# First layer and attention in nine blocks of 512 tokens instead of twelve of 384

## The chip, the cores and the metric

The kernel runs on one core of a Trainium2 chip. The metric is the device time of one execution in microseconds (us), without transfers from the host. The engines are TensorE (PE, its weight loads PEld), VectorE (DVE), ScalarE (ACT), GpSimd (POOL) and SyncE (SP, which issues all DMAs here).

## The reference

Attention over 8 batches of 8 heads, 576 tokens each, head width 64, with keys and values averaged over groups of 8 tokens (72 pooled rows per head), and then two expert layers over the 4608 tokens of width 512:

```python
k_p = k.reshape(B, H, Sp, pool, D).mean(axis=3)          # Sp = 72, pool = 8
v_p = v.reshape(B, H, Sp, pool, D).mean(axis=3)
scores = scale * np.matmul(q, k_p.transpose(0, 1, 3, 2))
scores = scores - np.max(scores, axis=-1, keepdims=True)
attn = np.exp(scores)
attn = attn / (np.sum(attn, axis=-1, keepdims=True) + 1e-09)
x = np.matmul(attn, v_p)                                 # -> 4608 x 512
h = x @ w_in; r = np.maximum(h, 0.0); x = (r * r) @ w_out         # first layer, d_ff 2048
gate = 1.0 / (1.0 + np.exp(-(x @ w_gate)))                        # second layer, d_ff 1536
out = (gate * (x @ w_val)) @ w_out2
```

The weights arrive as float64. The kernel turns them into float32 by integer operations on their halves.

## The kernel before

**Matmuls.** Each float32 operand of the two layers is split into a rounded high part and a remainder, and a product is three matmuls (high·high, high·low, low·high: `PASSES`). Tokens lie along the free dimension. In the first layer a block of `NA` = 384 tokens meets 16 slices `f` of the hidden width: `mm1` (line 791) makes the 128 hidden rows of slice `f` with 12 matmuls of 384 columns, ACT and DVE form the squared ReLU and split it (`relu`, `sq`, `ghi`, `glo`, lines 834 to 847), and `mm2` (line 800) adds their part of the output with 12 more. There are 12 blocks.

**Order of the blocks.** `SEGS` lists block 0 with slices 0 to 7, block 1 with all 16, block 0 with slices 8 to 15, and then blocks 2 to 11. So the 32 weight slices of the first layer are converted while the first two segments run. A conversion is a DMA, an integer addition on POOL, one ACT operation, four on DVE (lines 246 to 257) and a split on ACT and DVE (lines 273 and 277). The slices stay in SBUF for the whole layer.

**Attention.** For a block and half of the heads (`hf`), `attend` takes tiles of 128 tokens: scores on PE (line 443), maximum, exponential and scaling (`softmax1` to `softmax3`), a transposition of the result (on PE for blocks 0 and 1, line 528, by DVE and DMAs for the later ones, lines 511 and 522), and the product with the pooled values (line 544). A tile of block `b` holds the 32-token groups `a::NTA` of the block, a stride of three groups. From block 3 on, `softmax1` subtracts the maximum on DVE (line 467), one ACT operation takes the exponential of all four heads, and DVE sums. In the first three blocks (`FEW`) ACT takes it head by head, with the maximum as its bias and the sum as a by-product (line 496). Pooling of keys and values is done once per batch by DVE (line 381), or by PE for the first two batches (line 632).

**Second layer.** It works in blocks of 768 tokens with 384-column matmuls for the gate and value products (line 1181) and 512-column matmuls for the output (line 1296). It begins when the first layer ends.

**What sets the order.** Every operation is entered into `Plan` with an engine, a guessed duration, what it depends on, the buffers that it takes and gives, and a rank. `Plan.run` plays them through and so fixes the order of each engine's instructions; on the chip an engine works through its list in that order and waits where a semaphore isn't there yet. `T0` and `TF` are the planned start of the first layer and the planned length of a slice. Products of slice `f` are ranked `TI(f)` for `mm1` and 1.5 slices later for `mm2`, so that `mm2(f)` stands behind `mm1(f+1)`.

## Time and profile before

| | us |
|---|---|
| median of 3 runs (1782.91 to 1785.81) | 1784.85 |
| the profiled execution | 1785.78 |
| its span, first to last instruction | 1784.0 |
| PE busy in the span | 1752.6 (98%) |
| DVE busy | 1160.5 (65%) |
| ACT busy | 774.6 (43%) |
| mean granted clock of TensorE | 0.996 |

The span is what the trace covers; 1.8 us of the execution lie around it. A busy share is a mean over stages with different limits, so the rows below are taken stage by stage. Busy PE time contains the modelled end of each pipelined matmul: how fast a stream of matmuls really goes is read from the starts.

### The profile page before, as it was taken

How to read it: one execution, taken by the hardware profiler on the slowest of the kernel's cores; microseconds unless marked ns; L12 is line 12 of the kernel's file. 1: busy time of each engine (PE TensorE's matmuls, PEld its weight loads, DVE VectorE, ACT ScalarE, POOL GpSimd, SP SyncE). 2: the span in 40 equal slices, each digit the busy share in tenths (PEclk: the TensorE clock that was granted, in tenths of full speed). 3: DMA queues.
4: the chain of work that ended last, by engine and by line, in shares of the span. 5: the costliest groups of instructions: out<-in, count | busy, mean ns of one | idle time of the engine just before them, and what ended most of it. 6: DMA issues, size and time to landing. Idle time of an engine off the chain costs nothing.

```text
span 1784.0 us, 26488 instructions
## 1 busy us (share of the span) xinstructions
PE 1752.6 (98%) x9720; PEld 1636.1 (92%) x9720; DVE 1160.5 (65%) x2310; ACT 774.6 (43%) x1718; POOL 245.9 (14%) x186
## 2 busy tenths in 40 slices
PE   8898999999999999999999999999999999999999
PEld 3697889999999999999999999999999999999998
DVE  7999788788677886653357555555555655655554
ACT  6666533333333334333245444455444444444442
POOL 2500100000000000000023111212111212111100
PEclk9999999999999999999999999999999999999999
DMA  9632345343243442312022222223333333333321
GB/s 285 214 97 74 92 97 147 97 130 95 80 112 103 123 105 77 92 45 63 13 67 82 71 71 83 72 83 116 115 107 107 119 107 119 118 104 103 103 79 50
DMA packets 194658, 179.15 MB, mean 100 GB/s; under 512 B 105184, under 2 KB 143584, under 8 KB 194528
## 3 DMA queue, kind: packets, MB, share of 16 engines
q1 hardware_dynamic: 194528, 177.46, 33.8%
q8 instruction: 76, 1.25, 0.3%
q14 instruction: 54, 0.44, 0.1%
HBM read 119.80 MB, written 48.76 MB: 94 GB/s over the span
## 4 chain that ended last, share of the span: by engine, by line
PE 89%; DVE 3%; ACT 1%; DMA 1%; issue 1%; SPq 1%; POOL 0%; DVEq 0%; ACTq 0%; POOLq 0%
PE acc L800 20%; PE h L791 19%; PE h L1181 17%; PE acc L1296 17%; PE att L1181 8%; PE acc L1181 4%; PE att L544 2%; PE att L443 2%; DVE g L847 0%; DMA kv<-in_k_dram 0%; POOL raw L236 0%; SPq L427 0%; DVE kp L381 0%; DMA raw<-in_moe_w_out_dram 0%; DVE vp L381 0%
## 5 line engine op out<-in xcount | busy, mean ns | idle before, releaser
L791 PE MATMUL h<-x,in 128*128 128x384 f32 x2304 | 438.6, 339 | 7.9 <-DVE x L785 3.0
L800 PE MATMUL acc<-g,out 128*128 128x384 f32 x2304 | 439.3, 338 | 5.1 <-DVE g L847 2.5
L791 PEld LDWEIGHTS h<-x,in 128*128 128x128 f32 x2304 | 401.0, 189 | 19.4 <-issue 7.4
L800 PEld LDWEIGHTS acc<-g,out 128*128 128x128 f32 x2304 | 400.6, 188 | 18.1 <-DVE g L847 5.0
L834 ACT ACTIVATE r<-h 128x384 f32<-128x384 f32 x192 | 93.9, 489 | 262.1 <-PE h L791 257.0
L1296 PE MATMUL acc<-in,p 128*128 128x512 f32 x648 | 182.5, 390 | 0.0
L1296 PE MATMUL acc<-out,p 128*128 128x512 f32 x648 | 182.1, 389 | 0.0
L840 DVE TENSOR_TENSOR r<-r,h 128x384 f32<-128x384 f32 x160 | 87.8, 549 | 132.9 <-ACT r L834 131.9
L1203 ACT ACTIVATE res<-h 128x384 f32<-128x384 f32 x144 | 70.6, 491 | 211.3 <-PE h L1181 210.5
L844 ACT ACTIVATE g<-r 128x384 fp32r<-128x384 f32 x192 | 100.8, 525 | 108.5 <-DVE r L840 97.3
L1296 PEld LDWEIGHTS acc<-out,p 128*128 128x128 f32 x648 | 121.6, 188 | 25.7
L1296 PEld LDWEIGHTS acc<-in,p 128*128 128x128 f32 x648 | 121.4, 188 | 24.1
L847 DVE TENSOR_TENSOR g<-r,g 128x384 fp32r<-128x384 f32 x192 | 112.8, 587 | 42.8 <-ACT g L844 41.9
L236 POOL INT64_ADD raw<-raw x40 | 47.0, 1174 | 646.3 <-DMA raw<-in_moe_w_out_dram 176.6
L1212 DVE TENSOR_TENSOR res<-res,acc 128x384 f32<-128x384 f32 x72 | 39.7, 551 | 125.6 <-PE acc L1181 125.6
L1322 DVE TENSOR_TENSOR o<-o,acc 128x512 f32<-128x512 f32 x72 | 49.5, 688 | 94.9 <-PE acc L1296 74.1
L1262 ACT ACTIVATE p<-res 128x384 fp32r<-128x384 f32 x144 | 75.3, 523 | 70.8 <-DVE res L1256 70.6
L1014 POOL TENSOR_TENSOR yt<-yf,yt 128x768 f32<-128x768 f32 x32 | 62.1, 1942 | 273.6 <-DVE out L1041 272.3
L1181 PE MATMUL h<-out,in 128*128 128x384 f32 x432 | 98.4, 335 | 0.0
L1181 PE MATMUL h<-in,out 128*128 128x384 f32 x432 | 98.1, 334 | 0.3 <-DVE res L1212 0.3
L1181 PE MATMUL h<-in,in 128*128 128x384 f32 x432 | 98.1, 334 | 0.0
L1181 PE MATMUL h<-out,out 128*128 128x384 f32 x432 | 98.0, 334 | 0.0
(147 smaller groups left out, 2647.6 us busy)
## 6 DMA issues: line engine op xcount, KB each, us to landing
yf<-y_dram SPq DMA_DIRECT2D x16, 1536.0 KB
o_part<-o SPq DMA_DIRECT2D x72, 256.0 KB
o<-o_part SPq DMA_DIRECT2D x72, 256.0 KB
y_dram<-y SPq DMA_DIRECT2D x48, 192.0 KB
w_dram<-t SPq DMA_DIRECT2D x36, 256.0 KB
w2s<-w_dram SPq DMA_DIRECT2D x36, 256.0 KB
out_dram<-o SPq DMA_DIRECT2D x36, 256.0 KB
raw_w<-in_moe_w_in_dram SPq DMA_DIRECT2D x15, 512.0 KB
```

The lines of the kernel that those rows point to most:

```text
L791: nc.tensor.matmul(out=h[:, 0:n], lhsT=w[:, a, kk * 128:(kk + 1) * 128], rhs=xs[kk][:, c], start=(kk == 0 and i == 0), stop=(kk == KT - 1 ...
L800: nc.tensor.matmul(out=y_ps[m][:, 0:NA], lhsT=w[:, a, m * 128:(m + 1) * 128], rhs=g_t[f][:, c], start=(f == f0 and i == 0), stop=(f == f1 ...
L834: nc.scalar.activation(out=r, in_=st["h"][:, 0:NA], func=ACTF.Relu)
L840: nc.vector.tensor_tensor(out=st["r"], in0=st["r"], in1=st["h"][:, 0:NA], op=ALU.mult)
L844: nc.scalar.activation(out=g[:, 0], in_=st["r"], func=ACTF.Copy)
L847: nc.vector.tensor_tensor(out=g_t[f][:, 1], in0=st["r"], in1=g_t[f][:, 0].bitcast(F32), op=ALU.subtract)
L1014: nc.gpsimd.tensor_tensor(out=t, in0=q(a), in1=q(c), op=ALU.subtract)
L1181: nc.tensor.matmul(out=st[which, z][:, 0:HN], lhsT=w[:, wa, col:col + 128], rhs=ys[y, k2][:, yc], start=(first[z] == m and k2 == 0 and j = ...
L1203: nc.scalar.activation(out=new((which, key)), in_=st[which, z][:, 0:HN], func=ACTF.Copy)
L1262: nc.scalar.activation(out=p_t[fi][:, 0, h * HN:(h + 1) * HN], in_=st["gate", key], func=ACTF.Copy)
L1296: nc.tensor.matmul(out=o_ps[i], lhsT=p_t[f][:, a, i * 128:(i + 1) * 128], rhs=wslot[c, "out", f][:, w], start=(f == 0 and j == 0), stop=(f ...
L1322: nc.vector.tensor_tensor(out=st2["o"], in0=st2["o"], in1=o_ps[i], op=ALU.add)
```

## The change

`NA` becomes 512, so that there are nine blocks, and every matmul of the first layer has 512 columns. A tile of 128 tokens is now 128 adjacent tokens. Columns of a block stand in the order (32-token group, tile, token), which is undone when the block's output is copied out of PSUM (`tail_y`). Seven of the nine blocks lie in two batches; a tile that does is scored in two pieces, and `attn_v` walks the rectangles that `runs` returns. The softmax by heads on ACT is used for all blocks; the minus sign of the maximum comes from the reduction, and the scale is put into the keys when they are placed. `mm2(f)` is ranked 2.5 slices after `mm1(f)` and three buffers hold `g`. The planner's durations and lead times are adapted. The second layer keeps 384 columns (`HN`).

```diff
-    NA = 384
+    NA = 512
-    L2, L2H, LN, LNH, LP, LQ = 73.0, 31.0, 77.0, 35.0, 26.0, 18.0
+    L2, L2H, LN, LNH, LP, LQ = 92.0, 40.0, 96.0, 44.0, 26.0, 18.0
-    T0, TF, TG = 42.0, 4.25, 8.4
+    T0, TF = 44.0, 5.55
+    def runs(i, j):
+        res = []
+        if i % 128:
+            res.append((i % 128 // 32, 4, i // 128, i // 128 + 1))
+        if -(-i // 128) < j // 128:
+            res.append((0, 4, -(-i // 128), j // 128))
+        if j % 128:
+            res.append((0, j % 128 // 32, j // 128, j // 128 + 1))
+        return res
...
     def softmax1(b, hf, a):
...
-        nc.vector.tensor_reduce(out=m, in_=p, op=ALU.max, axis=AX.X)
-        nc.vector.tensor_scalar(out=m, in0=m, scalar1=-scale / POOL, scalar2=None, op0=ALU.mult)
+        nc.vector.tensor_reduce(out=m, in_=p, op=ALU.max, axis=AX.X, negate=True)
...
         for off, n, be, _ in parts(b):
-            for j in range(2):
-                nc.tensor.matmul(
-                    out=p[64 * j:64 * j + 64, off:off + n],
+            for g0, g1, a0, a1 in runs(off, off + n):
+                for j in range(2):
+                    nc.tensor.matmul(
+                        out=pv[64 * j:64 * j + 64, g0:g1, a0:a1],
...
-            if b < FEW:
-                o = op("dve", 0.57, lambda a=a: softmax1_few(b, hf, a), [o], r + 1)
-                o = op("act", 1.25, lambda a=a: softmax2_few(b, hf, a), [o], r + 2, give=(bank[0],))
-                o = op("dve", 0.78, lambda a=a: softmax3_few(b, hf, a), [o], r + 3)
-            else:
-                o = op("dve", 0.87, lambda a=a: softmax1(b, hf, a), [o], r + 1, give=(bank[0],))
-                o = op("act", 0.34, lambda a=a: softmax2(b, hf, a), [o], r + 2)
-                o = op("dve", 1.25, lambda a=a: softmax3(b, hf, a), [o], r + 3)
+            o = op("dve", 0.44, lambda a=a: softmax1(b, hf, a), [o], r + 1)
+            o = op("act", 2.0, lambda a=a: softmax2(b, hf, a), [o], r + 2, give=(bank[0],))
+            o = op("dve", 0.78, lambda a=a: softmax3(b, hf, a), [o], r + 3)
...
-            rank = t + 1.5 * TF
-            need = [o, w_ready["out", f]]
+            rank = t + 2.5 * TF
+            need = [o, w_ready["out", f]] + ([w_last["out", f - 1]] if f > f0 else [])
...
+            o_y = y.rearrange("p (a g t) -> p g a t", a=NTA, g=4)
+            i_y = y_ps[m].rearrange("p (g a t) -> p g a t", a=NTA, g=4)
-                nc.scalar.activation(out=y, in_=y_ps[m][:, 0:NA], func=ACTF.Copy)
+                nc.scalar.activation(out=o_y, in_=i_y, func=ACTF.Copy)
...
-    HN = NA
+    HN = 384
```

On PE, in block 1 (slices 3 to 5; `in_` and `out_` are the two weight slices, `acc` the four output banks), the list before has:

```order
L791 MATMUL h<-x,in_465 128x384 x12
L800 MATMUL acc_1173<-g,out_483 128x384 x3
L800 MATMUL acc_1182<-g,out_483 128x384 x3
L800 MATMUL acc_1191<-g,out_483 128x384 x3
L800 MATMUL acc_1198<-g,out_483 128x384 x3
L791 MATMUL h<-x,in_525 128x384 x12
```

and the list of the change, from slice 2 of the same block:

```order
L777 MATMUL h<-x,in_497 128x512 x12
L786 MATMUL acc_1286<-g,out_433 128x512 x3
L786 MATMUL acc_1294<-g,out_433 128x512 x3
L786 MATMUL acc_1300<-g,out_433 128x512 x3
L786 MATMUL acc_1310<-g,out_433 128x512 x3
L777 MATMUL h<-x,in_577 128x512 x12
```

Before, `out_483` is slice 2, right behind `mm1` of slice 3; now `out_433` is slice 0, behind `mm1` of slice 2. The matmuls have 512 columns where they had 384.

On DVE, at the end of the first segment, where the last weight that this segment needs (`w_out` of slice 7: `out_1038`, now `out_1065`) gets its remainder, the list before has:

```order
L785 TENSOR_TENSOR x<-xf,x 128x384 x2
L503 TENSOR_SCALAR z<-z 128x4
L504 RECIPROCAL z<-z 128x4
L505 TENSOR_TENSOR e_81<-e_81,z 128x4x72
L847 TENSOR_TENSOR g<-r,g 128x384
L277 TENSOR_TENSOR out_1038<-t_w,out_1038 128x512
```

and the list of the change:

```order
L771 TENSOR_TENSOR x<-xf,x 128x512
L256 SCALAR_TENSOR_TENSOR t_w<-raw_w,t_w 128x512
L833 TENSOR_TENSOR g<-r,g 128x512
L390 TENSOR_REDUCE kp<-kv 72x64
L771 TENSOR_TENSOR x<-xf,x 128x512
L276 TENSOR_TENSOR out_1065<-t_w,out_1065 128x512
```

The weight's place on DVE is nearly the same (row 160 before, row 158 now), while the block that it serves has a third more tokens.

On ACT, in a later block (`e_80` and `e_81` are the two buffers of a softmax tile), the list before has:

```order
L472 ACTIVATE e_80<-e_80 128x4x72
L834 ACTIVATE r<-h 128x384
L844 ACTIVATE g<-r 128x384
L834 ACTIVATE r<-h 128x384
L844 ACTIVATE g<-r 128x384
L472 ACTIVATE e_81<-e_81 128x4x72
```

and the list of the change:

```order
L486 ACTIVATE e_80,z<-att,m 128x72 x4
L820 ACTIVATE r<-h 128x512
L486 ACTIVATE e_81,z<-att,m 128x72 x4
L830 ACTIVATE g<-r 128x512
L403 ACTIVATE kpT_79<-att 64x72 x2
L820 ACTIVATE r<-h 128x512
```

One operation per tile has become four, ahead of a `relu` on which PE's next use of that bank depends.

## Rows read from the trace of the kernel before

**Rows 1.** Windows by stage: length, busy PE, PEld, DVE, ACT, POOL, clock, DMA.
```profile
0.00:38.88 38.88, 30.23 (x109) 13.14 (x109) 27.14 (x62) 23.26 (x78) 9.85 (x14) 0.96 1.09 279
38.88:102.64 63.76, 56.27 (x334) 45.86 (x331) 62.15 (x105) 45.86 (x125) 25.34 (x21) 0.95 0.59 191
102.64:180.91 78.27, 70.79 (x394) 67.34 (x392) 73.66 (x150) 48.59 (x118) 4.46 (x4) 0.98 0.37 95
180.91:224.21 43.30, 42.56 (x242) 38.80 (x243) 33.47 (x79) 23.95 (x64) 5.40 (x3) 1.00 0.31 82
224.21:958.31 734.10, 731.07 (x4319) 701.22 (x4319) 509.34 (x1068) 267.47 (x562) 59.60 (x54) 1.00 0.33 90
958.31:1784.00 825.69, 821.68 (x4333) 769.69 (x4332) 454.70 (x851) 365.49 (x775) 141.24 (x93) 1.00 0.30 96
```

**Rows 2.** Timeline of PE, first layer: start, length, what, count.
```profile
899.11 2.24 PE L791 MATMUL h<-x,in 128*128 128x384 f32 x12
...
944.87 2.24 PE L791 MATMUL h<-x,in 128*128 128x384 f32 x12
```

**Rows 3.** Timeline of PE, output products of the second layer.
```profile
992.19 0.84 PE L1296 MATMUL acc<-out,p 128*128 128x512 f32 x3
...
998.99 0.84 PE L1296 MATMUL acc<-out,p 128*128 128x512 f32 x3
```

**Rows 4.** Waits of PE, 38.88 to 102.64: total, times, longest.
```profile
PE att L443 <- ACT qT L716: 2.9, 1, 2.9
PE att L528 <- DVE e L505: 1.9, 1, 1.9
PE h L791 <- DVE x L785: 1.8, 1, 1.8
```

**Rows 5.** Waits of PE, 102.64 to 224.21.
```profile
PE h L791 <- DVE in L277: 2.1, 3, 1.0
PE h L791 <- ACT in L273: 2.1, 2, 1.5
PE acc L800 <- ACT out L273: 1.7, 1, 1.7
```

**Rows 6.** Waits of PE, 224.21 to 958.31.
```profile
PE acc L800 <- DVE g L847: 2.5, 6, 0.7
```

**Rows 7.** Windows in the start, up to the last conversions: columns as rows 1.
```profile
24.55:100.10 75.55, 66.85 (x366) 50.32 (x364) 73.08 (x133) 54.84 (x159) 28.58 (x23) 0.93 0.71 215
100.10:191.92 91.82, 83.39 (x471) 78.66 (x469) 85.16 (x176) 58.75 (x151) 7.77 (x4) 0.98 0.34 88
```

**Rows 8.** Lines of DVE, 24.5 to 102.64: count, busy us, mean ns, idle before.
```profile
L252 DVE SCALAR_TENSOR_TENSOR t_w<-raw_w,t_w 128x512 uint32<-128x512 uint32 x14 | 12.1, 864 | 0.1
...
L847 DVE TENSOR_TENSOR g<-r,g 128x384 fp32r<-128x384 f32 x8 | 6.1, 759 | 0.1
L277 DVE TENSOR_TENSOR out<-t_w,out 128x512 fp32r<-128x512 f32 x8 | 5.4, 681 | 0.0
L505 DVE TENSOR_TENSOR e<-e,z 128x288 f32<-128x288 f32 x9 | 4.7, 524 | 0.3
L381 DVE TENSOR_REDUCE kp<-kv 72x64 f32<-72x512 f32 x4 | 4.2, 1058 | 0.0
```

**Rows 9.** Timeline of PE: scores, two tiles, in halves and whole.
```profile
71.10 1.20 PE L443 MATMUL att<-kpT,qT 128*64 128x144 f32 x16
...
162.99 1.14 PE L443 MATMUL att<-kpT,qT 128*128 128x144 f32 x8
```

**Rows 10.** Timeline of PE: the product with the values, halves and whole.
```profile
101.19 1.52 PE L544 MATMUL att<-aT,vp 72*64 72x192 f32 x16 [0.21 <-ACT aT L536]
...
829.35 1.51 PE L544 MATMUL att<-aT,vp 72*64 72x384 f32 x8
```

**Rows 11.** Timeline of ACT: a tile's four exponentials, and what follows.
```profile
140.97 0.32 ACT L496 ACTIVATE e<-att,m 128x72 f32<-128x72 f32 x1 [1.12 <-DVE m L487]
...
142.30 0.49 ACT L834 ACTIVATE r<-h 128x384 f32<-128x384 f32 x1
```

**Rows 12.** Lines of DVE, 224.21 to 890: the subtraction that goes.
```profile
L467 DVE TENSOR_TENSOR e<-att,m 128x288 f32<-128x288 f32 x49 | 22.4, 458 | 1.7
```

More of the change, by code (lines that the diff above doesn't have):

```diff
@@ L160 @@
     scale = 1.0 / float(D) ** 0.5
+    kscale = scale / POOL
     def pool(name, bufs=1, **kw):
@@ L404, in prep @@
                              take=("kp",) if j == 0 else (), give=("kv",)))
-            o = op("pe", 0.12, lambda pr=pr: tr(pr), ds, rank, take=("att",), give=("kp",), at=0)
             prev = k_users[be - 2, 2 * hf + pr]
+            o = op("pe", 0.12, lambda pr=pr: tr(pr), ds + prev, rank, take=("att",), give=("kp",), at=0)
             k_ready[be, 2 * hf + pr] = op("act", 0.25, lambda pr=pr: place(pr), [o] + prev, rank, give=("att",))
@@ L434, in q_trans @@
         for pr in range(2):
-            nc.vector.transpose(out=qT_t[b, hf][:, pr, a], in_=q_t[b, hf][:, pr, a::NTA, :])
+            nc.vector.transpose(out=qT_t[b, hf][:, pr, a], in_=q_t[b, hf][:, pr, 4 * a:4 * a + 4, :])
     def scores(b, hf, a, bank):
@@ L441, in scores @@
             for off, n, be, _ in parts(b):
-                p0, pn = off * 128 // NA, n * 128 // NA
+                p0, p1 = max(0, off - 128 * a), min(128, off + n - 128 * a)
+                pn = p1 - p0
+                if pn <= 0:
+                    continue
                 nc.tensor.matmul(
@@ L455, in new_e @@
         if u % 2 == 0:
-            e_first[0] = moe.tile([128, 2, 4 * 96], F32, tag="g", name="e", bufs=2)
+            e_first[0] = moe.tile([128, 2, 4 * 96], F32, tag="g", name="e", bufs=3)
         return e_first[0][:, u % 2]
@@ L496, in softmax2_few, with softmax3 @@
             nc.scalar.activation(
-                out=e[:, h, 0:SP], in_=p[:, h * SP:(h + 1) * SP], func=ACTF.Exp, scale=scale / POOL,
+                out=e[:, h, 0:SP], in_=p[:, h * SP:(h + 1) * SP], func=ACTF.Exp,
                 bias=m[:, h:h + 1], accum_out=z[:, h:h + 1])
-    def softmax3_few(b, hf, a):
+    def softmax3(b, hf, a):
         e = e_view(b, hf, a)[:, :, 0:SP]
@@ L520, in a_move @@
             nc.sync.dma_start(
[L521 removed]
+                out=aT_t[b, hf][32 * j:32 * j + w, :, NG * g:NG * (g + 1)],
                 in_=T_t[b, hf][32 * g:32 * g + w, :, j].rearrange("p h a t -> p h (a t)"))
@@ L716, in ev @@
                 nc.scalar.activation(
-                    out=out_of(pr).rearrange("p a g t -> p g a t"),
-                    in_=st["p"][:, 0:NA].rearrange("p (g a t) -> p g a t", g=4, a=NTA), func=ACTF.Copy)
-            o = op("pe", 0.4, tr, loads[NTA * (pr // 2):NTA * (pr // 2 + 1)] + consts, rank + 5 + pr, take=(bank[0],),
+                    out=out_of(pr).rearrange("p a g t -> p (a g t)"), in_=st["p"], func=ACTF.Copy)
+            o = op("pe", 0.5, tr, loads[NTA * (pr // 2):NTA * (pr // 2 + 1)] + consts, rank + 5 + pr, take=(bank[0],),
                    give=takes if pr == KT - 1 else ())
-            res.append(op("act", 0.37, ev, [o], rank + 6 + pr, take=(out_take(pr),) if out_take(pr) else (),
+            res.append(op("act", 0.58, ev, [o], rank + 6 + pr, take=(out_take(pr),) if out_take(pr) else (),
                           give=(bank[0],)))
@@ L757 @@
     q1 = early_q(1, t1 - Q1, 0.5,
-                 [lambda: att.tile([128, 2, H, D], F32, tag="T", name="rows1"),
-                  lambda: att.tile([128, 1, H, D], F32, tag="kv", name="rows1", bufs=3)],
-                 ("T", "kv"), q1_out, lambda pr: {0: "qT", 2: "q"}.get(pr), [("att", 2)] * KT, [c1])
+                 [q0_get(-2), q0_get(-1)], (w1_tag(n1 - 4), w1_tag(n1 - 3)), q1_out, lambda pr: {0: "qT", 2: "q"}.get(pr), [("att", 2)] * KT, [c1])
     early_kv(1, v, n1 - 11, t1 - P1 + V1L, K1B, [c2], False)
@@ L808, in expert1 @@
         for kk in range(KT):
-            o = op("act", 0.41, lambda kk=kk: x_hi(b, kk), [x_kept[b, kk]], t0 - 60, take=(f"x{kk}",))
-            xr.append(op("dve", 0.47, lambda kk=kk: x_lo(b, kk), [o], t0 - 60, give=((f"xf{kk}", xf_owner[b, kk]),)))
+            o = op("act", 0.6, lambda kk=kk: x_hi(b, kk), [x_kept[b, kk]], t0 - 60, take=(f"x{kk}",))
+            xr.append(op("dve", 0.67, lambda kk=kk: x_lo(b, kk), [o], t0 - 60, give=((f"xf{kk}", xf_owner[b, kk]),)))
         for f in range(f0, f1):
@@ L825, in expert1 @@
                 for kk in range(KT):
-                    o = op("pe", 0.52, lambda kk=kk, l1=l1: l1([kk]), [o, xr[kk], w_ready["in", f]], t,
+                    o = op("pe", 0.68, lambda kk=kk, l1=l1: l1([kk]), [o, xr[kk], w_ready["in", f]], t,
                            take=("h",) if kk == 0 else (), give=give if kk == KT - 1 else ())
             else:
-                o = op("pe", 2.08, lambda l1=l1: l1(range(KT)), [w_ready["in", f]] + xr, t, take=("h",), give=give)
+                o = op("pe", 2.72, lambda l1=l1: l1(range(KT)), [w_ready["in", f]] + xr, t, take=("h",), give=give)
             w_last["in", f] = o
@@ L867, in expert1 @@
             else:
-                o = op("pe", 2.08, lambda f=f: [mm2(f, f0, f1, m) for m in range(KT)], need, rank, give=("g",))
+                o = op("pe", 2.72, lambda f=f: [mm2(f, f0, f1, m) for m in range(KT)], need, rank, give=("g",))
             w_last["out", f] = o
@@ L978, in y_prep @@
         st = {}
-        blks = {x for x in range(t0 // NA, (t0 + TN) // NA)}
+        blks = {x for x in range(t0 // NA, -(-(t0 + TN) // NA))}
         def load():
```

70 lines of the change are left out of this document (26 added, 44 removed).

## The prediction, on record before the changed kernel ran

> **What bounds the kernel now.** I read the windows by stage first, then the starts of PE's matmuls in each stage, PE's waits, and last the lines of DVE and ACT for the stage that waits. The windows [rows 1] are cut where PE's work changes: 38.88 is the first matmul of the first layer, 102.64 lies in the last products of segment 0, 180.91 in the first ones of segment 2, 224.21 is the start of block 2, and 958.31 the first matmul of the second layer. From 224.21 on the reader is to see a PE that hardly rests: 731.1 of 734.1 us and 821.7 of 825.7 busy, at granted clock 1.00. What counts there is the number of matmuls and the time from one start to the next. The start is another matter. Between 38.88 and 224.21 PE is idle for 7.5 + 7.5 + 0.7 = 15.7 us, and the granted clock is 0.95 and 0.98 in the first two windows, which by itself can cost at most 63.8 x 0.05 + 78.3 x 0.02 = 4.8 us. Its waits there are for queries, a scaled softmax tile, the split x and for weight slices [rows 4, 5], all of which come from DVE or from ACT operations that feed it or are fed by it. DVE is the engine without air: 73.1 of 75.6 us up to the remainder of the weight that segment 0 needs last, 85.2 of 91.8 us from there to the last weight [rows 7]. Part of its work is stretched there: the bit operation at line 252 has a mean of 864 ns and the split at line 847 one of 759 [rows 8].
>
> **The change part by part.**
>
> *Matmuls of the first layer.* In a run of products without attention, 22 groups of 12 lie between the two starts shown: (944.87 - 899.11) / 264 = 173.3 ns for 384 columns [rows 2]. The output products of the second layer have 512 columns and another weight tile for each matmul too, as the first layer will: (998.99 - 992.19) / 30 = 226.7 ns [rows 3]. At the full clock of 2.4 GHz, 384 columns are 160.0 ns and 512 are 213.3, so both carry the same 13.3 ns on top, and a third more columns cost 30.8% more time. Before there are 12 x 16 x 24 = 4608 matmuls, 798.7 us; now 9 x 16 x 24 = 3456, 783.4 us. This term is **-15.3 us**, all of it on the path, since PE is the bound for most of the layer.
>
> The Trainium skill has a rule that speaks against this term (page "TensorE: Matmul & The Clock Gate", section "Back-to-back issue gap"): for a single warm stream the gap is the columns at 2.4 GHz plus about 2.5 ns. By it, as an estimate, 1152 matmuls fewer would give 2.9 us and not 15.3, and the sum below would end some 12 us higher. This case's trace disagrees with its size: it has 13.3 ns at both widths [rows 2, 3]. I go by the rows.
>
> *The start: segment 0.* DVE's list up to the last weight of segment 0 has 158 places where it had 160. In it are one key pooling more (1.06 us), two more softmax tiles to scale (0.52 each) with their maxima, eight splits of g and six of x that are a third longer (at most 8 x 0.25 us for g, somewhat less in all for x), and twelve small multiplications of the maxima less [rows 8]. Bounds are +2 and +7 us; I take +6, nearer the upper one, because the list is worked off without a gap. PE's own work in this segment grows by 192 x (226.7 - 173.3) = 10.2 us and by some 2.4 us for two more tiles of attention, an estimate from the length of such groups [rows 9, 10]. So PE gets 12.6 us more work in a stage that DVE lengthens by 6: its waits and cold time shrink by **6.6 us**, from 7.5 idle and up to 3.2 of clock. The number of weights doesn't change; what changes is that each, once there, gives PE a third more to do.
>
> *The start: segments 1 and 2.* Here PE waits 8.2 us, mostly for weights [rows 1, 5]. DVE needs 91.8 us for the last sixteen slices [rows 7], and its list is 153 places long now against 157, with two longer kinds in it: say 97 us. PE's work over segment 1 goes from 66.6 to 87.0 us plus attention (4.2 us before: 78.3 - 7.5 - 66.6; 5.6 with a third more). PE thus comes to the weights later than DVE has them, up to the last two or three, and there the second product helps, which stands behind two further first products. I leave 2.5 us of waits: **-5.7 us**. The ends are 0 and, with all clock loss gone, -9.8.
>
> *Before the first matmul.* Block 0 has eight tiles to go through softmax instead of six, and the first half of the heads, with which `mm1` can begin, needs four where it needed three. One more set of four exponentials for each half of the heads, 142.30 - 140.97 = 1.33 us on ACT [rows 11], lies on this path with its maximum and scaling: bounds 0 (PE has pooling to do meanwhile) and +4; I take **+2**.
>
> *Attention on PE.* The number of tiles stays 72 and so do the columns of the value product. A tile in two pieces costs the same as a whole one (1.20 and 1.14 us for two tiles), and a value product in halves as much as a whole one (1.52 and 1.51) [rows 9, 10]. But `runs` now makes pieces of 64 columns, which the trace doesn't show: two in each of blocks 1, 3, 5 and 7, times four (half and head pair), 32 pairs. The 16 pieces in rows 9 take 1.20 us, 75 ns each for 144 columns; by columns a piece of 64 would need 33 ns. If it can't follow its neighbour faster than those 75 ns, a pair of heads with two passes each loses 4 x 42 ns, 5.4 us in all. The other end is 0, or a little below since value products are grouped into 18 rounds and not 24. I take **+1**.
>
> *DVE and ACT later on.* The subtraction (458 ns a tile [rows 12]) and two reductions leave DVE, four exponentials with their sums instead of one come to ACT, 1.33 us a tile. DVE has 509 of 734 us busy and ACT 267 after 224.21 [rows 1], and what hides both is PE's stream. PE's waits there are 2.5 us, for g [rows 6]. With the second product a slice later g has 12 x 226.7 x 2 = 5.4 us more time, so these waits could go; new ones at block starts are as likely. Cost 0, bounds -3.0 and the slower rival below. DMAs for attention move the same bytes in fewer pieces, off the path. The second layer is left as it is: 0.
>
> *Sum*: -15.3 - 6.6 - 5.7 + 2 + 1 = -24.6 us. From the profiled execution, 1785.8 us, that is 1761.2; the median of the runs is 0.9 lower than this execution, and I forecast **1761 us**.
>
> **The rivals.**
>
> *The start gives nothing.* DVE's chain of conversions stretches with the block (longer splits, more tiles) and PE finds the same holes. For it: DVE is over 90% busy throughout the start. Against it: the number of weight operations is fixed, and they are most of the list. Time: 1785.8 - 15.3 + 2 + 1 = 1773.5 us. Chance 14%.
>
> *The cost goes by columns.* If the first layer's matmuls kept their 451 ns per thousand columns, 512 columns would take 231.1 ns, the term of 15.3 us would vanish, and the time be 1776 us. For it: the first layer's own stream at 512 columns is in no row. Against it: rows 3, with the same operand types. Chance 4%. By the gap rule of the Trainium skill (page "TensorE: Matmul & The Clock Gate", section "Back-to-back issue gap"), as an estimate, 12.4 of the 15.3 us would be missing, which is close to this case.
>
> *More than forecast.* All idle and cold time of the start goes and so do the later waits: -15.3 - 20.5 - 3.0 = -38.8, or 1747; a middle of this case is 1751. Chance 8%.
>
> *Slower: the exponentials hold PE.* From block 3 on there are 48 tiles whose bank of scores is now held until ACT has done its four exponentials, and each set stands ahead of a `relu` on ACT's list. If PE then finds the h bank or the scores' bank taken, it waits. The price: PE must lose (24.6 + 3.6) / 48 = 0.59 us a tile before the kernel is slower by 0.2%; at 0.65 us a tile the time is 1792 us. For it: ACT's list shows the four operations ahead of `relu`. Against it: in the first three blocks the same form runs, at 1.33 us a tile, and no wait there is for it as large [rows 4, 5]; and the bank that `relu` and the square free is needed again only after three further groups of twelve, 3 x 2.72 = 8.2 us. Chance 4%.
>
> That the matmuls don't get their 512 columns is excluded by the instruction list.
>
> **How the numbers follow.** The forecast has 70%, its own range is 1754 to 1769: the bounds of segment 0, of the pieces and of the first matmul add up to about 7 on either side. The others have 14, 4, 8 and 4. To leave out no more than 2 in 10 the range takes in the case without a gain in the start, the one by columns with its own scatter, and most of the low case: 1750 to 1779. A change under 0.2%, 3.6 us, can hardly be told from none for this kernel. All cases but the last are faster by more than that; for pieces that add up worse than thought I move a few points: faster 0.93, the same 0.03, slower 0.04.
>
> **What would show it.** The first layer's two matmul lines with 1728 entries each, 2.72 us from one group of twelve to the next; PE's idle time between its first matmul of the first layer and the start of block 2 at 3 to 6 us, where it was 15.7; that first matmul at 39 to 42 us; the last products of segment 0 at about 108; and the first matmul of the second layer at 934 rather than 958. DVE should lose some tens of microseconds of busy time and ACT gain some, without either showing in the end. The prediction is wrong if groups of twelve take 2.77 us, if PE's waits in the start stay at 15 us with DVE's weights as their cause, or if after the start waits for ACT's exponentials or for `relu` appear in tens of microseconds.

## The result and the profile after

The changed kernel takes 1765.93 us (median of 4 runs, 1764.18 to 1766.26) against 1785.03 us of the kernel before on the same chip. The ratio is 0.9893, with a 95% interval of 0.9876 to 0.991. The forecast was 1761 us in a range of 1750 to 1779. The profiled execution took 1764.18 us with a span of 1762.4, so the span fell by 21.6 us where the working had 24.6. Several terms of that working were off by more than 3 us, in both directions, and most of what follows is about those.

The windows by stage of the changed kernel (length; busy PE, PEld, DVE, ACT, POOL; granted clock, DMA share, GB/s) answer to [rows 1]. The cuts are the first matmul of the first layer, the end of segment 0, the start of block 2, and the first matmul of the second layer:

```profile
0.00:41.24 41.24, 31.08 (x122) 15.46 (x123) 21.97 (x51) 23.13 (x88) 11.29 (x15) 0.96 1.07 271
41.24:117.09 75.85, 70.47 (x335) 49.25 (x333) 70.58 (x118) 55.85 (x146) 25.07 (x19) 0.95 0.49 166
117.09:261.25 144.16, 141.36 (x661) 113.13 (x659) 105.30 (x215) 87.47 (x224) 7.24 (x6) 0.98 0.32 83
261.25:926.78 665.53, 665.08 (x3168) 539.38 (x3167) 438.40 (x824) 272.37 (x744) 59.68 (x54) 1.00 0.35 96
926.78:1762.40 835.62, 827.79 (x4345) 774.79 (x4343) 455.84 (x853) 366.25 (x775) 139.09 (x92) 0.99 0.29 96
```

Read the first column against the second. From 261.25 to 926.78 PE rests 0.45 us in all; before it rested 3.0 us in the same part of the kernel. In the start it still rests 5.4 + 2.8 us, where it was 7.5 + 8.2. And the second layer, which nobody touched, is 835.6 us long and was 825.7.

The timeline of PE in a run of products (start, length, line, what, count) answers to [rows 2]:

```profile
869.66 2.88 PE L786 MATMUL acc<-g,out 128*128 128x512 f32 x12
872.38 2.88 PE L777 MATMUL h<-x,in 128*128 128x512 f32 x12
875.10 2.88 PE L786 MATMUL acc<-g,out 128*128 128x512 f32 x12
```

From one start to the next it is 2.72 us, 226.7 ns a matmul. Each of the two lines has 1728 entries in the list of groups.

The waits of PE from 41.24 to 261.25 (total, times, longest), which answer to [rows 4, 5]:

```profile
PE h L777 <- DVE x L771: 3.3, 1, 3.3
PE att L518 <- DVE e L495: 2.3, 3, 1.7
PE att L518 <- ACT qT L705: 0.9, 1, 0.9
PE att L537 <- ACT aT L526: 0.9, 1, 0.9
PE h L777 <- DVE in L276: 0.7, 1, 0.7
```

The waits for weights have shrunk from 5.9 us [rows 5] to 0.7. The largest wait is one of the first slice's matmuls for the split of x, 3.3 us from 51.6 on; before it was 1.8 [rows 4]. After 261.25 there is one wait of 0.4 us; the 2.5 us for g [rows 6] are gone.

Two groups of attention in the timeline of PE, a score product of two whole tiles and a value product of 32 pieces, answer to [rows 9, 10]:

```profile
421.43 1.14 PE L455 MATMUL att<-kpT,qT 128*128 128x144 f32 x8
474.23 1.99 PE L537 MATMUL att<-aT,vp 72*64 72x256 f32 x32
```

The 32 pieces of the second row (16 of them of 64 columns, though the row prints one form) cover 512 tokens of the block in 1.99 us; before, 384 tokens took 1.51 [rows 10], and a third more of that is 2.01.

### The profile page after: what moved, and what is told of

Its sections match the earlier page's. It is cut to its first block, busy times and chain, and to the rows that moved or that the text cites. A ratio compares the mean times of both kernels' runs of the same rounds, so it can differ in the third digit from the quotient of the medians.

```text
span 1762.4 us, 24051 instructions
## 1 busy us (share of the span) xinstructions
PE 1735.8 (98%) x8624; PEld 1492.0 (85%) x8624; DVE 1092.1 (62%) x2058; ACT 805.1 (46%) x1974; POOL 242.4 (14%) x186
## 4 chain that ended last, share of the span: by engine, by line
PE 93%; DMA 1%; DVE 0%; ACT 0%; issue 0%; SPq 0%; ACTq 0%
PE h L777 22%; PE acc L786 21%; PE h L1169 17%; PE acc L1284 17%; PE att L1169 9%; PE acc L1169 4%; PE att L537 2%; PE att L455 2%; DMA y_dram<-y 0%; DVE vp L390 0%; DMA q<-in_q_dram 0%; PE att L399 0%; PE att L518 0%; DVE in L276 0%; DVE y L868 0%
## 5 line engine op out<-in xcount | busy, mean ns | idle before, releaser
L777 PE MATMUL h<-x,in 128*128 128x512 f32 x1728 | 427.0, 396 | 4.3 <-DVE x L771 3.7
L786 PE MATMUL acc<-g,out 128*128 128x512 f32 x1728 | 421.7, 393 | 0.0
L777 PEld LDWEIGHTS h<-x,in 128*128 128x128 f32 x1728 | 323.1, 189 | 79.6 <-DVE x L771 5.1
L786 PEld LDWEIGHTS acc<-g,out 128*128 128x128 f32 x1728 | 321.3, 188 | 70.7 <-issue 3.9
L820 ACT ACTIVATE r<-h 128x512 f32<-128x512 f32 x144 | 86.1, 598 | 268.7 <-PE h L777 262.8
L826 DVE TENSOR_TENSOR r<-r,h 128x512 f32<-128x512 f32 x112 | 76.5, 683 | 131.1 <-ACT r L820 130.8
L833 DVE TENSOR_TENSOR g<-r,g 128x512 fp32r<-128x512 f32 x144 | 102.6, 713 | 52.7 <-ACT g L830 51.6
L830 ACT ACTIVATE g<-r 128x512 fp32r<-128x512 f32 x144 | 91.1, 633 | 69.4 <-DVE r L826 67.6
L1169 PE MATMUL h<-in,in 128*128 128x384 f32 x432 | 99.3, 337 | 3.8 <-ACT res L1191 3.8
L486 ACT ACTIVATE e<-att,m 128x72 f32<-128x72 f32 x272 | 83.3, 321 | 39.9 <-DVE m L477 39.7
```

Of the source, the lines that this page charges most:

```text
L486: nc.scalar.activation(out=e[:, h, 0:SP], in_=p[:, h * SP:(h + 1) * SP], func=ACTF.Exp, bias=m[:, h:h + 1], accum_out=z[:, h:h + 1])
L777: nc.tensor.matmul(out=h[:, 0:n], lhsT=w[:, a, kk * 128:(kk + 1) * 128], rhs=xs[kk][:, c], start=(kk == 0 and i == 0), stop=(kk == KT - 1 ...
L786: nc.tensor.matmul(out=y_ps[m][:, 0:NA], lhsT=w[:, a, m * 128:(m + 1) * 128], rhs=g_t[f][:, c], start=(f == f0 and i == 0), stop=(f == f1 ...
L820: nc.scalar.activation(out=r, in_=st["h"][:, 0:NA], func=ACTF.Relu)
L826: nc.vector.tensor_tensor(out=st["r"], in0=st["r"], in1=st["h"][:, 0:NA], op=ALU.mult)
L830: nc.scalar.activation(out=g[:, 0], in_=st["r"], func=ACTF.Copy)
```

## The experiments

Each run was compared with the kernel before on its own chip, whose median lay between 1784.9 and 1786.2 us. "After" is the changed kernel, 1765.93 us.

**What the matmuls cost.** In `e2_cols256` each matmul of `mm1` becomes two of 256 columns, so there are 1728 matmuls more and the columns stay the same. (The two halves share one accumulation, so the hidden rows have other values.)

```diff
-            nc.tensor.matmul(
-                out=h[:, 0:n], lhsT=w[:, a, ...], rhs=xs[kk][:, c], ...)
+            for s in (slice(0, n // 2), slice(n // 2, n)):
+                nc.tensor.matmul(
+                    out=h[:, s], lhsT=w[:, a, ...], rhs=xs[kk][:, c, s], ...)
```

> The changed kernel with each matmul of mm1 issued as two of 256 columns: 1728 more matmuls, the same columns. Theory (about 13.3 us per thousand matmuls, whatever their width): a pair takes 240 ns where one took 226.7, +23 us against the changed kernel, 1789 us. Rival (the cost goes by columns): no change, 1766 us. With a fixed cost of 2.5 ns a matmul it would be +4 us, 1770 us.

Measured: 1785.61 us (ratio 1.0002, 0.9991 to 1.0013), 19.7 more than after. Blocks 3 to 7, from the first matmul of block 3 to that of block 8, are windows in which PE doesn't rest at all; first after, then this run:

```profile
362.69:839.74 477.05, 477.05 (x2268) 385.96 (x2267) 300.88 (x579) 188.86 (x519) 36.92 (x34) 1.00 0.35 97
```

```profile
369.40:858.76 489.36, 489.36 (x3228) 437.06 (x3227) 301.01 (x581) 188.57 (x519) 36.02 (x33) 1.00 0.35 95
```

960 matmuls more cost 12.3 us, 12.8 ns each, at clock 1.00 in both. So a matmul has a fixed price of about 13 ns beside its columns, as [rows 2, 3] had it, and the rival by columns falls. The 19.7 us over the whole kernel are a little under the theory's 23. The 2.5 ns that the Trainium skill gives (page "TensorE: Matmul & The Clock Gate", section "Back-to-back issue gap") are there the price of an isolated matmul; for a stream with a weight load for each matmul, as here, the section lets both count and has some 131 ns at 512 columns. The prediction left that out. The 226.7 ns measured here agree with neither figure, and the measurement decides.

**What the later second product is worth.** `e3_lag15` takes the lag back in the changed kernel; `e5_before_lag25` gives it to the kernel before, with a third buffer for g.

```diff
 (e3, in after)                     (e5, in before)
-            rank = t + 2.5 * TF    -            rank = t + 1.5 * TF
+            rank = t + 1.5 * TF    +            rank = t + 2.5 * TF
```

> The changed kernel with the second product ranked 1.5 slices after the first again instead of 2.5 (three buffers of g stay). Theory (most of the gain at the start comes from more matmul work per weight, and in the later blocks the waits for g were 2.5 us before): +1 to +4 us against the changed kernel, 1767 to 1770 us, with waits of the second product for g's remainder or for weights. Rival (the later second product is what hides the start): +6 us or more, with the time lost ahead of block 2.

> Twelve blocks of 384 tokens and the old softmax, as before; only the second product stands 2.5 slices behind the first one (1.5 before), with a third buffer for g. Theory (the longer lag is what fills the holes of segments 1 and 2, whatever the block size): PE's idle time between its first matmul of the first layer and block 2 falls from 15.7 us to 8 or less, block 2 starts some 6 to 8 us earlier than at 224.21, the waits for g after that (2.5 us) go, and the handoff to the second layer is some 6 us longer, as in the run that took the lag back; time 1777 to 1783 us. Rival (the larger block fills the holes, because each weight gives PE a third more to do; the lag alone moves nothing): block 2 starts at 222 to 226, time 1783 to 1790 us.

`e3_lag15`: 1768.62 us (0.9901, 0.9884 to 0.9918). Its windows, with the first two stages in one:

```profile
41.42:269.04 227.62, 219.17 (x1015) 167.58 (x1013) 180.84 (x346) 144.70 (x374) 32.18 (x25) 0.96 0.38 110
269.04:938.21 669.17, 666.01 (x3161) 539.79 (x3159) 436.99 (x814) 271.36 (x741) 60.69 (x54) 1.00 0.34 95
938.21:1766.89 828.68, 822.88 (x4333) 769.83 (x4331) 453.51 (x849) 364.71 (x773) 139.37 (x92) 1.00 0.30 96
```

Against after this is +7.6 in the start, +3.6 up to the second layer, and -6.9 in the second layer. After leaves two groups of twelve matmuls for the next stage, this run one, at block 2 and again at the second layer; so 2.7 us of each outer difference only changed sides. Without them the lag is worth 4.9 + 3.6 us ahead of the border between the layers and costs 4.2 behind it. By the medians, 2.7 us, the theory's +1 to +4 holds, but the time is lost ahead of block 2, as the rival had it. It is not lost in waits: PE rests 8.5 us in this start and 8.2 in after. The three largest waits of PE in it are

```profile
PE att L455 <- ACT qT L705: 2.9, 1, 2.9
PE att L518 <- DVE e L495: 2.5, 1, 2.5
PE h L777 <- DVE x L771: 1.6, 2, 1.0
```

and none is for a weight. Part of the 4.9 us is clock (granted 0.96, in after 0.97 over the same stage); the rest was not followed up.

`e5_before_lag25`: 1784.14 us (0.9994, 0.998 to 1.0007), no difference. Its start:

```profile
37.89:107.50 69.61, 61.04 (x349) 50.11 (x347) 65.26 (x108) 48.26 (x131) 30.25 (x21) 0.93 0.58 186
107.50:226.31 118.81, 108.86 (x607) 103.46 (x605) 102.84 (x219) 68.98 (x174) 6.69 (x6) 0.97 0.33 88
```

PE still rests 8.6 + 10.0 us there, and its largest waits in the second window, three with 5.1 us in all, are for `out` weights. The theory fell: with blocks of 384 tokens the lag fills nothing. As `e3_lag15` has no wait for a weight with the short lag, it is the longer block, a third more to do for each weight, that makes these waits go.

**What DVE's conversions and GpSimd's additions do to the start.** Two kernels take work out of the 32 weight conversions with the order of all else kept: `e7_after_light` two of DVE's four steps, `e10_no_int64` the 64-bit addition on GpSimd. `e11_before_no_int64` does the latter to the kernel before.

```diff
 (e10, e11)
         def round24():
             raw = s["raw"]
-            nc.gpsimd.int64_add(raw, raw, ROUND_AND_REBIAS)
 (e7)
-        for fn, d in ((b1, 0.4), (b2, 0.4), (b3, 0.66)):
+        for fn, d in ((b1, 0.4), (skip, 0.4), (skip, 0.66)):
```

> The changed kernel with two of the four DVE steps (the shift and the operation on the sign bit) left out of each of the 32 weight conversions of the first layer, the order of everything else kept; the weights then have other values. It takes some 32 x 1.1 = 35 us from DVE in the start. Theory (DVE's list sets the pace of segment 0 in the changed kernel, which ended at 117.1 where I had it at 108): the last products of segment 0 end at 105 to 111, block 2 starts 6 to 12 us earlier than at 261.25, and the time falls by as much, to 1754 to 1761 us. Rival (ACT, GpSimd or the transfers pace the conversions): segment 0 ends after 114 and the time is 1763 to 1767 us.

> The changed kernel with GpSimd's 64-bit addition left out of each of the 32 weight conversions of the first layer, the order of everything else kept; the weights then have other values. DVE's work is the same instruction for instruction. Theory (GpSimd's additions stretch DVE's operations in the start, 1.0 to 1.5 us where the same forms take 0.42 to 0.68): the DVE operations on 128x512 words that start between 46 and 58 us have their short durations, DVE's busy time up to block 2 falls by 10 us or more, segment 0 ends at 107 to 113 and the time is 1755 to 1762 us. Rival (the stretch comes from something else, such as bank or transfer traffic): DVE's durations and its busy time stay within 3 us, time 1763 to 1767 us.

> The kernel before, twelve blocks of 384, with GpSimd's 64-bit addition left out of each of the 32 weight conversions of the first layer (the weights then have other values). In the changed kernel this took 12 us off. Theory (the collision of GpSimd and DVE is a property of the conversions and costs both kernels alike): PE's idle time up to block 2, 15.7 us, falls to 5 or less, block 2 starts 8 to 14 us earlier than at 224.21, time 1771 to 1778; the change would then be worth about as much as with the additions, 18 to 23 us. Rival (the collision grew with the change, since the longer segment brought it under PE's path): the time falls by 5 us or less, to 1779 to 1784.

`e7_after_light`: 1756.39 us (0.9838, 0.982 to 0.9855). Segment 0 ends at 109.96, block 2 starts at 253.42, 7.8 us earlier than in after, all inside what its theory said.

`e10_no_int64`: 1753.69 us (0.982, 0.9804 to 0.9837), 12.2 less than after, where its theory had 1755 to 1762. Its segment 0, and below it that of `e11_before_no_int64`:

```profile
40.13:106.79 66.66, 66.62 (x336) 48.25 (x333) 56.45 (x118) 55.47 (x146) 0.00 (x0) 1.00 0.58 191
```

```profile
35.78:89.98 54.20, 53.99 (x344) 45.48 (x342) 48.42 (x108) 47.25 (x130) 0.00 (x0) 1.00 0.81 254
```

DVE does the same 118 operations as in after and is busy 56.45 us, where it was 70.58. So 14.1 us of DVE's busy time in that window went with the additions. The lines of DVE by form in segment 0 show it (count, busy, mean ns, idle before); first after, then `e10_no_int64`, whose line numbers are one higher:

```profile
L251 DVE SCALAR_TENSOR_TENSOR t_w<-raw_w,t_w 128x512 uint32<-128x512 uint32 x14 | 12.1, 861 | 0.1
L245 DVE TENSOR_SCALAR t_w<-t_w 128x512 f32<-128x512 f32 x14 | 8.9, 639 | 2.2 <-ACT t_w L241 2.2
L390 DVE TENSOR_REDUCE kp<-kv 72x64 f32<-72x512 f32 x4 | 4.3, 1064 | 0.0
L771 DVE TENSOR_TENSOR x<-xf,x 128x512 fp32r<-128x512 f32 x4 | 3.6, 889 | 0.0
```

```profile
L252 DVE SCALAR_TENSOR_TENSOR t_w<-raw_w,t_w 128x512 uint32<-128x512 uint32 x14 | 9.6, 684 | 0.0
L246 DVE TENSOR_SCALAR t_w<-t_w 128x512 f32<-128x512 f32 x14 | 5.9, 422 | 2.3 <-ACT t_w L242 2.2
L391 DVE TENSOR_REDUCE kp<-kv 72x64 f32<-72x512 f32 x4 | 4.3, 1064 | 0.0
L772 DVE TENSOR_TENSOR x<-xf,x 128x512 fp32r<-128x512 f32 x4 | 2.7, 685 | 0.0
```

With GpSimd's additions, operations with two tensors in SBUF go from 684 to 861 or 889 ns, those with one tensor and a constant from 422 to 639; the pooling, a reduction, stays at 1064. That agrees with a rule of the Trainium skill (page "SBUF — State Buffer", section "SBUF: two separate sides"): GpSimd and DVE share a pair of ports, which one of them locks for a whole instruction, and on DVE's side only operations with two SBUF inputs or in a mode that uses both ports are held up. That the operations with a constant run in such a mode, no run here shows.

Leaving the addition out also takes a step out of each conversion. In after ACT, which does the next step, waits only 0.3 us for GpSimd between 41.24 and 261.25, so there the step itself is worth next to nothing and DVE's stretch is what counts. In the kernel before ACT waits 6.6 us for it up to block 2, and the two are not told apart.

In the kernel before the addition costs still more, 1768.73 us without it (0.9907, 0.9883 to 0.9931), 17.4 less than before on the same chip. The theory had 8 to 14 and expected the change's worth to stay. Without the additions the change is worth 1768.73 - 1753.69 = 15.0 us, with them 19.1. By the medians part of the gain thus was that the longer block hides more of a collision that both kernels have; the intervals of the ratios are too wide to exclude that the worth is the same.

**What the softmax on ACT is worth.** `e4_old_softmax` restores the subtraction and the sum on DVE from block 3 on.

```diff
+            if b < 3:
                 o = op("dve", 0.44, lambda a=a: softmax1(b, hf, a), [o], r + 1)
...
+            else:
+                o = op("dve", 0.87, lambda a=a: softmax1_old(b, hf, a), [o], r + 1, give=(bank[0],))
+                o = op("act", 0.34, lambda a=a: softmax2_old(b, hf, a), [o], r + 2)
+                o = op("dve", 1.25, lambda a=a: softmax3_old(b, hf, a), [o], r + 3)
```

> The changed kernel with the former softmax from block 3 on: maximum, subtraction and sum on DVE, one exponential for four heads on ACT (the scale stays in the keys). Theory (PE is the bound there and neither engine shows): within 2 us of the changed kernel, 1764 to 1768 us, DVE busy 40 to 60 us more and ACT less. Rival (DVE's relief is part of the gain): +4 us or more, as waits of PE for g or x in blocks 3 to 8.

Measured: 1771.31 us (0.9922, 0.9902 to 0.9942), 5.4 more than after. The window from block 2 to the second layer, and the two largest waits of PE in it:

```profile
261.64:933.67 672.03, 666.30 (x3161) 539.61 (x3160) 476.81 (x914) 232.17 (x431) 60.48 (x54) 1.00 0.35 95
```

```profile
PE h L803 <- DVE x L797: 2.8, 4, 1.2
PE acc L812 <- DVE g L859: 1.9, 1, 1.9
```

It is 6.5 us longer than after's 665.53, DVE is busy 38 us more, and PE rests 5.7 us, 4.7 of them for x and g, which DVE splits. The theory fell, and the rival's +4 us or more holds.

**Where the second layer's 10 us went.** The border is the first matmul of the second layer. `y` is the first layer's output on its way to DRAM, `res` a partial sum of the second layer that ACT copies out of PSUM. In after, PE works on two left-over groups of `mm2` among the first products of the second layer (24 matmuls, 5.44 us; before one group, 2.08). Then, in the timeline of PE:

```profile
935.87 0.69 PE L1169 MATMUL acc<-in,in 128*128 128x384 f32 x3
...
942.69 1.33 PE L1169 MATMUL h<-in,in 128*128 128x384 f32 x3 [3.83 <-ACT res L1191]
943.81 1.16 PE L1169 MATMUL h<-out,in 128*128 128x384 f32 x3
944.77 1.16 PE L1169 MATMUL h<-in,in 128*128 128x384 f32 x3
945.73 1.16 PE L1169 MATMUL h<-out,in 128*128 128x384 f32 x3
```

and in that of ACT:

```profile
942.14 0.87 ACT L1191 ACTIVATE res<-h 128x384 f32<-128x384 f32 x2 [3.79 <-DMA y_dram<-y]
```

ACT doesn't write `res` until a store of y has left, as if the `res` tiles lay on the memory of the last y tiles; before there is no such wait. After it, groups of three matmuls stand 0.96 us apart instead of 0.52, and the window from 942.69 to 948.48 has a granted clock of 0.51, the lower level of 1.2 GHz. `e1_res_free` puts a spare tile under `res`; `e8_last15_free` adds a lag of 1.5 slices for the last block alone.

```diff
+            if "pad" not in bp:
+                bp["pad"] = bp["l"].tile([128, 4096], F32, tag="pad", name="pad")
 (e8 also)
-            rank = t + 2.5 * TF
+            rank = t + (1.5 if b == NBLK - 1 else 2.5) * TF
```

> The changed kernel with one edit: 16 KB per partition are left unused ahead of the second layer's res tiles, so that none of them lies where the last block's output tiles wait for their stores. Theory (the wait at the start of the second layer, 3.8 us on ACT's copy into res and some 2.7 us of matmuls at half clock behind it, comes from shared memory): both go, about -6.5 us against the changed kernel, 1759 to 1760 us, ratio to before about 0.986; the six groups of three after the wait take 0.52 us each again. Rival (ACT is simply late there, behind the copies of the last outputs): the wait stays within 1 us of 3.8 and the time within 1 us of 1766.

> The changed kernel with two edits for the handoff to the second layer: the second product stands 1.5 slices behind in the last block alone, so that one group of twelve instead of two is left at the end, and a spare tile moves the tiles `res` off the y tiles whose stores are still under way. Theory (the two edits add up: the lag in the last block gives back the 3.4 us of matmuls, the tile another 2.6 us as measured): second layer 828 to 831 us long where it was 835.6, first matmul of the second layer at 926 to 928, time 1758 to 1762 us. Rival (the handoff waits for something that neither edit moves, such as the subtractions on GpSimd, and the lag's loss only moves ahead of the border): second layer no shorter than 832, time 1763 to 1766 us.

`e1_res_free`: 1763.31 us (0.9871, 0.985 to 0.9892), second layer 832.75 us. ACT's wait is gone, so it did come from the shared memory, but PE now waits 1.8 us for a DVE addition into `res`: 2.6 us came back of the 6.5 that I expected. DVE and GpSimd in that place, in this run:

```profile
943.92 1.89 DVE L1246 TENSOR_TENSOR res<-res 128x384 f32<-128x384 f32 x1 [1.83 <-ACT res L1242]
945.73 0.54 DVE L1202 TENSOR_TENSOR res<-res,att 128x384 f32<-128x384 f32 x1
946.40 1.51 DVE L1256 TENSOR_TENSOR p<-res,p 128x384 fp32r<-128x384 f32 x1
```

```profile
943.54 1.85 POOL L1002 TENSOR_TENSOR yt<-yf 128x768 f32<-128x768 f32 x1 [17.17 <-DMA yf<-y_dram]
945.47 2.02 POOL L1002 TENSOR_TENSOR yt<-yf,yt 128x768 f32<-128x768 f32 x1
```

The two long DVE operations have two SBUF inputs and lie beside GpSimd's subtractions; the addition from PSUM between them takes its 0.54.

`e8_last15_free`: 1762.21 us (0.9866, 0.9849 to 0.9883). The last block of the first layer, and the second layer:

```profile
842.21:933.57 91.36, 90.05 (x397) 74.27 (x396) 49.77 (x69) 35.53 (x65) 18.79 (x16) 1.00 0.16 52
933.57:1761.01 827.44, 822.82 (x4333) 769.89 (x4331) 455.82 (x849) 364.45 (x773) 139.30 (x92) 1.00 0.29 97
```

The second layer is 5.3 us shorter than in `e1_res_free`, but the last block takes 91.36 us where it took 87.04 in after (839.74 to 926.78): 4.3 of them only moved ahead of the border, 2.7 as a group of twelve and 1.3 as a wait for g. My figure of 926 to 928 for the first matmul of the second layer was wrong for that reason, and the two edits don't add up: the rival's half about the lag holds, its 832 us for the second layer doesn't.

`e12_late_sub_lag25` and `e9_late_sub` were to hold GpSimd's subtractions back in `e1_res_free` and `e8_last15_free`, by one more dependency in the planner:

```diff
-        make("T1", "B12", "B11", ld)
+        ldT = ld + list(hold)
+        make("T1", "B12", "B11", ldT)
...
-            y_prep(nxt[1], t + BT, t)
+            y_prep(nxt[1], t + BT, t, [p_ready[1, 1]] if step == 0 else ())
```

> The changed kernel with the spare tile that moves `res` off the y tiles, and GpSimd's subtractions for the second step of the second layer held until DVE has written the last remainder of the first group of products. Before, with the tile alone, PE still waited 1.8 us at the handoff for a DVE addition, two of whose predecessors took 1.9 and 1.5 us (0.55 elsewhere) while GpSimd subtracted, and went on at half clock for some 3.5 us. Theory (these GpSimd subtractions stretch DVE there): DVE's operations between 940 and 952 us take 0.55 us each, PE's wait for `res` goes, the second layer takes 828.5 to 831 us (832.75 with the tile alone), time 1759 to 1762. Rival (DVE is stretched there by something else, or the wait merely moves): second layer 832 to 834, time 1762.5 to 1765.

> The same two edits, and the second product 1.5 slices behind in the last block alone. With those last two edits together PE still waited 0.9 us for `res`, and a DVE operation of 2.2 us lay beside GpSimd's subtractions. Theory: DVE's operations are back at 0.55 us, no wait over 0.3 us is left at the handoff, the second layer takes 825 to 827 us (827.4 before this edit), time 1759 to 1762, no better than with the lag of 2.5 everywhere, because the lag of 1.5 costs the last block what it gives back. Rival (the two add up): time below 1758.5.

1762.95 us (0.9875, 0.9854 to 0.9897) and 1762.01 us (0.9872, 0.985 to 0.9895). The subtractions ran where they had been, as GpSimd's timeline of `e12_late_sub_lag25` shows:

```profile
945.74 1.85 POOL L1002 TENSOR_TENSOR yt<-yf 128x768 f32<-128x768 f32 x1 [17.19 <-DMA yf<-y_dram]
```

The wait of 1.8 us for `res` was there again. The lists of the engines were the same as without the added dependency, so it moved nothing. The two runs tell nothing of the theory; they are repeats of `e1_res_free` and `e8_last15_free`. (The repeat of `e1_res_free` has no half clock behind the wait and a second layer of 831.19 us; the 1.6 us between them are an estimate of what that clock cost.) `e13_hold_sub` makes it a true wait, on `e1_res_free`:

```diff
+                if hold and name == "T1":
+                    nc.gpsimd.tensor_copy(out=t[:, 0, :], in_=p_t[1][:, 1, HN:TN].bitcast(F32))
                 nc.gpsimd.tensor_tensor(out=t, in0=q(a), in1=q(c), op=ALU.subtract)
```

> The changed kernel with the spare tile under `res`, and this time a true wait for GpSimd: ahead of its first subtraction for the second step it copies 128x384 words of the tile `p` that DVE writes last in the first group of products (some 955 us). The earlier edit gave only the planner a later time and moved no instruction: the subtractions still ran from 945.7 on. Theory (GpSimd's subtractions stretch DVE at the handoff): no subtraction runs between 943 and 953 us, DVE's two operations of 1.9 and 1.5 us take 0.55 each, PE's wait of 1.8 us for `res` falls to 0.5 or less, the second layer takes 829 to 831.5 us (832.75 and 831.2 in the two runs without the wait), time 1760 to 1762.5. Rival (something else stretches DVE there, such as ACT's table load or the transfers): DVE's durations stay above 1.2 us and PE's wait above 1.2.

1761.74 us (0.9868, 0.9852 to 0.9884). The same operations of DVE, and GpSimd:

```profile
943.86 0.56 DVE L1249 TENSOR_TENSOR res<-res 128x384 f32<-128x384 f32 x1 [1.83 <-ACT res L1245]
944.75 0.55 DVE L1205 TENSOR_TENSOR res<-res,att 128x384 f32<-128x384 f32 x1 [0.33 <-ACT res L1196]
945.22 0.55 DVE L1259 TENSOR_TENSOR p<-res,p 128x384 fp32r<-128x384 f32 x1
```

```profile
950.00 0.51 POOL L1003 COPY yt<-p 128x384 f32<-128x384 f32 x1 [23.67 <-DVE p L1259]
950.59 2.03 POOL L1004 TENSOR_TENSOR yt<-yf 128x768 f32<-128x768 f32 x1
```

1.89 and 1.51 us became 0.56 and 0.55 and PE's wait fell to 0.3, as its theory had it; the subtractions came back at 950.6, earlier than the 953 that it asked for. With this the stretch of DVE at the border is shown to come from GpSimd. That the hold saves time is not shown: the second layer has 831.4 us, inside the theory's range, but 831.19 in the repeat of `e1_res_free` without it, and PE waits 1.0 us for DVE's output tiles of the second layer, for which it didn't wait there. By medians this kernel and `e8_last15_free` are some 4 us below the changed one; the intervals of their ratios still overlap with its own.

## Why the prediction was right, and where it was not

The largest term, the matmuls, was right in size and in reason, and so was the end of the waits for weights. That the sum of all came within 3 us of the span is luck beside that: four terms were off by +4.3, +6.5, -8.0 and -2.6 us, and these nearly cancel. Of the signs, PE's rest in the start (8.2 us, not 3 to 6) and the end of segment 0 (117, not 108) missed too.

| term (us) | forecast | measured |
|---|---|---|
| matmuls of the first layer | -15.3 | -15.3 |
| segment 0: waits and cold time | -6.6 | -2.3 |
| segments 1 and 2: waits | -5.7 | -5.4 |
| before the first matmul | +2 | +2.4 |
| half clock in segments 1 and 2 | 0 | +1.3 |
| attention on PE (an estimate) | +1 | -7.0 |
| DVE and ACT later on | 0 | -2.6 |
| second layer | 0 | +6.5 |
| not assigned | | +0.8 |
| span | -24.6 | -21.6 |

*Matmuls.* 1152 fewer at 13.3 ns each, with 226.7 ns a matmul at 512 columns, came out as forecast, and `e2_cols256` shows the price by itself.

*Segment 0.* This is the step that failed first. I wrote that PE gets 12.6 us more work "in a stage that DVE lengthens by 6". From the first matmul to the end of the last second product at about 104.4 it took 65.5 us, and now 75.9: it grew by 10.3, so only 2.3 us of the holes were filled. The 12.6 was right: without the additions, where PE doesn't rest in either kernel, the stage grows by 66.66 - 54.20 = 12.5 us. The 6 was not. The same stage before, columns as in [rows 1]:

```profile
38.88:104.42 65.54, 58.05 (x344) 47.61 (x341) 63.53 (x108) 47.61 (x129) 25.34 (x21) 0.95 0.59 192
```

DVE's busy time grew by 7.1 us to 70.58, the upper bound, and its rest from 2.0 to 5.3 us, where I had a list "worked off without a gap": it waits 2.2 us for ACT's step of a conversion, 1.7 for exponentials and 1.3 for scores. The cold time didn't shrink either, at a granted clock of 0.95 in both. And DVE paces the stage for a reason that I had missed: 14.1 us of its busy time in after, and 63.53 - 48.42 = 15.1 before, are GpSimd holding it up. [rows 8] had it on show, 864 ns for an operation that takes 684; I noted the stretch and didn't ask who caused it. Being nearly alike in both kernels, it doesn't by itself explain the miss from 6 to 10.3. PE's wait of 3.3 us for the split of x, though, is gone in `e10_no_int64`.

*Segments 1 and 2.* Forecast 2.5 us of waits left, measured 2.8. The reason given, that PE comes to the weights later, stands: with the short lag no wait for a weight is left in the longer block either (`e3_lag15`), and the lag alone does nothing (`e5_before_lag25`). The later second product, on which I counted too, isn't needed for it. I had no term for the half clock, which grew (78.3 x 0.02 = 1.6 us before, 144.2 x 0.02 = 2.9 after, by the granted clocks).

*Before the first matmul.* 41.24 is inside the 39 to 42 forecast; the other runs of this start lay between 40.3 and 44.1, so that this term has some 2 us of scatter.

*Attention on PE.* From the first matmul of the first layer to that of the second it is 919.4 us before and 885.5 after. Take off the products (4596 at 173.3 and 3432 at 226.7 ns), PE's rest (18.7 and 8.6 us) and the clock (4.8 and 6.7 by the granted clocks): 99.3 us of attention and pooling are left before, and 92.3 after. That is 7.0 us less, an estimate, since the clocks are given to a hundredth; I had +1. The fear of pieces of 64 columns was groundless: in the group at 474.23 eight of them stand between the starts at 474.716 and 474.947, 29 ns each, below the lower end of 33 that I had set. Which part of the saving is fewer rounds and which longer ones wasn't tested.

*DVE and ACT later on.* I called the relief of DVE free because PE's stream hides both engines. PE's rest after block 2 fell from 3.0 to 0.45, and `e4_old_softmax` shows that the longer blocks without that relief would rest 5.7 and be 6.5 us longer. It belongs to the gain.

*Second layer.* "The second layer is left as it is: 0" overlooked that the border moves. Its 9.9 us more hold 3.4 us of `mm2` that only changed sides (part of the reason why its first matmul came at 926.8 and not at 934). Some 4.3 us went when `res` was moved off the y tiles (831.19 us in the repeat of `e1_res_free`, 832.75 in that run itself, 831.4 with the subtractions held). The remaining 2.3 us stay open.

The rivals: the one by columns and the slower one by the exponentials are out, the waits of the latter not being there at all. "The start gives nothing" was near the truth for segment 0, with 2.3 of the 6.6 us.

## What to carry to other kernels

Larger tiles pay a fixed price less often, here 13 ns a matmul, and this part of a forecast can be read off the starts of an existing stream of the target width. Where the profile shows an engine busy all the time, first compare its operations with the same forms elsewhere in the trace: the longer means were not work here but another engine's doing, and they went when that engine's work was left out or moved. And look at the stage borders of the parts that are left as they are: buffers that come to lie on others and half-finished groups that cross the border cost 6.5 us here, on a term that I had put at 0.

## What the runs showed of the hardware

- GpSimd's 64-bit additions cost 12.2 us of the changed kernel and 17.4 us of the one before (there with ACT's waits for them), though GpSimd was busy for only a third of segment 0 (25.07 of 75.85 us). DVE's operations with two tensors in SBUF took 861 to 889 ns beside them, 684 without, and a reduction 1064 with and without.
- After a wait of 3.8 us the granted clock over the next 5.8 us was 0.51, about 1.2 GHz, and groups of three matmuls took 0.96 us for 0.52. In `e1_res_free` a wait of 1.8 us was followed by groups of 0.96 too, in its repeat a wait of the same length was not.
- Value products of 64 columns stood 29 ns apart in the mean, in a group of 32 pieces that took 1.99 us for 512 tokens; whole products took 1.51 for 384.
